# The mask's identity product of a fused attention and mixture-of-experts kernel, in four tiles of 32 rows

## Chip, cores and metric

The kernel runs on one core of a Trainium2 chip. The metric is the time of one execution on the device in microseconds (us). TensorE is called PE below, its weight loads PEld; VectorE is DVE, ScalarE ACT, GpSimd POOL, and SyncE, which issues most DMAs, SP.

## What is computed

Attention over 8 batches with 8 heads of 576 tokens and 64 dimensions, masked to a window, then a mixture of 8 experts with a capacity of 80 tokens each:

```python
scores = scale * np.matmul(q, k.transpose(0, 1, 3, 2))
mask_plain = (rel >= 0) & (rel < window)                                  # window 32, heads 0 to 3
mask_dil = (rel >= 0) & (rel < window * dilation) & (rel % dilation == 0) # dilation 4, heads 4 to 7
scores = np.where(masks[None, :, :, :], scores, -1000000000.0)
attn = softmax(scores)
x = np.matmul(attn, v)            # 4608 tokens of 512
...
logits = x @ w_gate               # one expert per token, the 80 best tokens of each
h = np.maximum(x[tok_idx] @ w1[e], 0.0)
out[tok_idx] = gate_w[tok_idx, None] * (h @ w2[e])
```

(`attn = softmax(scores)` stands for the four lines of the maximum, exponential, sum and division.)

## The kernel before

The attention is cut into 36 tiles. One tile holds four blocks of 32 queries for each of the two kinds of heads; the 128 partitions are four groups g of 32, and on the free axis lie 4 blocks j x 2 heads x 64 keys, 512 columns of f32, one bank of PSUM (tag `sc`, three of them). Since a query sees only 32 keys back (for dilated heads in reordered positions), 64 keys suffice.

For each tile t, `scores(t)` issues two things on PE. First the mask: `identb`, a 128x128 identity in bf16, times `mask`, a bf16 tile of 0 and -8e9 with 4 x 64 columns that is read twice by a broadcast over the two heads. This product (line 350) starts the accumulation and so writes the mask into the bank. Then 16 products of queries and keys (line 354), each 32 rows of the output by 128 columns, add the scores: for each block j the four groups g. In f32 each of them is two records of PE and two of PEld in the profile.

After it come `smax` (DVE, maximum per row, line 360), `sneg` (POOL), `sexp` (ACT, eight exponentials, line 368), `ptrans` (DVE, transposes in 32x32, line 373), `pv` (PE, weights times values; line 405 for the regular tiles, 416 for the last ones), `raw` (ACT copies out of PSUM, line 425), `norm_r` and `norm` (DVE and POOL, lines 429 to 436), `xtrans` (PE transposes with the f32 identity, line 442), and copies on ACT. x goes to DRAM by a DMA on SP.

Between the tiles PE also does the routing of batches that are complete: `gate` (lines 521 to 542), `counts` (comparing keys: `KLp`, line 638, and `csp`, line 690) and `merge` (lines 754 to 801). After the last tile the routing of the last batch runs alone, with `warm` products (line 289) in between, and thirteen `fill` products of 512 columns. Then come the experts (line 1089), with their weights loaded ahead.

The order on every engine is fixed in the program: a planner (`drive`) takes from the chains of tiles and batches whichever step has the lowest cost by a table of estimated durations. In it `scores` is one step of PE. Queries, keys, values, masks and weights are loaded by SP at fixed places of that order (`before_scores`, `after_scores`).

Of the kernel before, what the change touches and what calls it, by code (L numbers as in the profile page):

```python
# [27 lines left out]
P = 128  # L28
# [91 lines left out]
def moe_attn_kernel(ctx: ExitStack, tc: tile.TileContext, io, dims, sig):  # L120
    nc = tc.nc
# [3 lines left out]
    NG = H // 2  # L125
    NT = N // P
    TPP = 2 * S // P
# [12 lines left out]
    out = io["out"]  # L140
# [8 lines left out]
    def const(name, dt=F32, pool=None):  # L149
        a = io[name]  # L150
        return (pool or cp).tile(list(a.shape), dt, name=f"c_{name}")
# [100 lines left out]
    with ExitStack() as c2:  # L252
# [13 lines left out]
        mask = kp.tile([P, TPP, 4, 64], BF16, name="mask")  # L266
        identb = const("identb", BF16, kp)
# [54 lines left out]
        t = 0  # L322
        while t < NT:
# [5 lines left out]
            t = e  # L329
# [16 lines left out]
        def scores(t):  # L346

            q = q2[t // 2 % NQ][:, t % 2]
            ps = ps2.tile([P, 4, 2, 64], F32, tag="sc", name=f"sc_{t}", bufs=3)
            nc.tensor.matmul(out=ps, lhsT=identb, rhs=mask[:, t % TPP].unsqueeze(2).broadcast_to([P, 4, 2, 64]), start=True, stop=False, skip_group_check=True)  # L350
            for j in range(4):
                for g in range(NG):
                    b, k = qplan[t][g // 2][j]
                    nc.tensor.matmul(out=ps[32 * g:32 * g + 32, j], lhsT=q[:, g, 32 * j:32 * j + 32], rhs=k2[b % 2][:, :, g, 32 * k:32 * k + 64],  # L354
                                     start=False, stop=True, skip_group_check=True)
            st[t] = {"sc": ps.rearrange("p j h c -> p (j h) c")}
# [547 lines left out]
        def tile_chain(t):  # L904
# [5 lines left out]
            e = yield "PE.sc", d_sc, max(qstart.get(t, 0.0), E_(("ex", t - 3)) + lat)  # L910
            before_scores(t)
            scores(t)
            after_scores(t)
            ev["sc", t] = e
# [126 lines left out]
        t = ps1.tile([P, 512], F32, tag="lt", name="fill")  # L1041
# [252 lines left out]
```

## Time and profile before

| | |
|---|---|
| median of three runs | 313.79 us (312.93 to 313.81) |
| the profiled execution | 311.25 us |
| its span | 309.5 us |
| mean granted clock of PE | 0.987 |

The profile is of one execution. It lists what each engine did when, in us from the start of the span, and names for an idle time what ended it. In names of tiles buffer numbers are left out. A form such as 128*32 behind a PE record is the part of the array that it uses, 128 rows by 32 columns; 128x512 behind it is what is streamed through. Ends of matmuls are modelled, starts are not, so intervals between starts say more than busy time.

### The profile page before, as it was taken

What the parts mean: (1) busy time and instruction counts of PE and PEld (TensorE: products, weight loads), DVE (VectorE), ACT (ScalarE), POOL (GpSimd) and SP (SyncE); (2) the same over time, 40 slices, a digit from 0 to 9 for tenths busy, and PEclk for the clock granted to TensorE, in tenths of its full rate; (3) what the DMA queues carried; (4) which work ended last, traced back from release to release, by engine and by line L of the source; (5) the groups of instructions that cost most, each with busy time, mean ns of one, the idle gap of its engine ahead of it and who ended that gap; (6) DMA issues with size and microseconds to landing.
All of it is one profiled execution on the core that took longest, in us unless ns stands there. A gap on an engine that the chain in (4) does not pass through costs nothing. (4 is left out here: it accounts for less than half of the span.)

```text
span 309.5 us, 12133 instructions
## 1 busy us (share of the span) xinstructions
PE 285.7 (92%) x4976; PEld 201.2 (65%) x4976; DVE 133.4 (43%) x532; ACT 162.3 (52%) x602; POOL 128.5 (42%) x273
## 2 busy tenths in 40 slices
PE   7659999999999999999899888889999999999991
PEld 6435566565575656665566666654788788788791
DVE  6424444768656857567587559840000000000000
ACT  3939777767757678678556754202232332332322
POOL 9503332646376484754286662446203321110111
PEclk9779999999999999999999999999999999999999
DMA  7999989979799998999985947957999999990000
GB/s 214 272 318 300 301 312 301 359 236 317 242 309 327 294 334 257 304 360 322 321 302 158 399 145 251 344 213 208 391 400 414 389 385 391 409 384 21 23 19 26
DMA packets 30727, 87.21 MB, mean 282 GB/s; under 512 B 4304, under 2 KB 6608, under 8 KB 29776
## 3 DMA queue, kind: packets, MB, share of 16 engines
q1 hardware_dynamic: 28832, 83.55, 78.5%
q0 software_dynamic: 1280, 2.62, 2.7%
q8 instruction: 39, 0.64, 0.9%
q10 hardware_dynamic: 560, 0.26, 0.4%
q14 instruction: 16, 0.13, 0.1%
HBM read 66.23 MB, written 20.19 MB: 279 GB/s over the span
## 5 line engine op out<-in xcount | busy, mean ns | idle before, releaser
L436 POOL TENSOR_TENSOR x<-r,rc 128x256 f32<-128x256 f32 x71 | 43.5, 634 | 59.4 <-DVE rc L430 17.5
L405 PE MATMUL pv<-v,pts 128*32 128x260 f32 x992 | 65.3, 387 | 0.1
L368 ACT ACTIVATE ex<-sc,mx 128x64 f32<-128x64 f32 x288 | 62.8, 344 | 3.4 <-POOL mx L363 3.4
L1089 PE MATMUL h<-wr,xe 128*32 128x256 f32 (+1 forms) x576 | 45.4, 452 | 0.7 <-ACT xe L1086 0.4
L467 ACT COPY xT<-xt 128x256 f32<-128x256 f32 (+5 forms) x114 | 33.5, 409 | 20.3 <-PE xt L442 20.3
L354 PE MATMUL sc<-k,q 128*32 128x128 f32 x1152 | 40.3, 282 | 3.8 <-issue 2.2
L1089 PE MATMUL y<-wr,hT 128*32 128x384 f32 (+1 forms) x768 | 43.5, 379 | 0.0
L1089 PEld LDWEIGHTS y<-wr,hT 128*32 128x32 f32 x768 | 42.3, 110 | 1.2 <-issue 0.2
L373 DVE STREAM_TRANSPOSE pts<-ex 128x512 f32<-128x512 f32 x36 | 25.4, 706 | 36.7 <-PE pv L405 26.7
L1119 DVE COPY hT<-th 128x192 f32<-128x192 f32 x8 | 2.9, 357 | 86.8 <-ACT hT L1122 86.8
L405 PEld LDWEIGHTS pv<-v,pts 128*32 128x32 f32 x992 | 27.9, 109 | 17.6 <-issue 3.5
L354 PEld LDWEIGHTS sc<-k,q 128*32 128x32 f32 x1152 | 30.4, 112 | 12.8 <-issue 8.3
L1144 POOL DMA_INDIRECT out<-yo,itok x8 | 7.4, 928 | 68.3 <-ACT yo L1141 51.7
L1089 PEld LDWEIGHTS h<-wr,xe 128*32 128x32 f32 x576 | 26.5, 110 | 13.7 <-ACT h L1107 0.8
L425 ACT COPY r<-pv 128x260 f32<-128x260 f32 x72 | 27.4, 425 | 14.3 <-PE pv L405 12.7
L360 DVE TENSOR_REDUCE mx<-sc 128x8 f32<-128x512 f32 x36 | 24.4, 679 | 13.1 <-PE sc L354 12.9
L442 PE MATMUL xt<-c_ident,x 128*128 128x128 f32 x144 | 23.6, 285 | 0.7 <-POOL x L436 0.4
L1138 ACT ACTIVATE yo<-y,gsel 80x384 f32<-80x384 f32 x8 | 4.6, 577 | 33.9 <-PE y L1089 33.9
L245 POOL DMA_INDIRECT xg<-xs,irow x16 | 15.6, 974 | 15.1 <-PE tx L1083 6.1
L442 PEld LDWEIGHTS xt<-c_ident,x 128*128 128x128 f32 x144 | 15.2, 141 | 8.2 <-issue 3.7
L717 POOL TENSOR_SCALAR or<-c_pack,rr 80x80 bf16<-80x80 f32 x40 | 18.8, 485 | 3.9 <-DVE rr L735 3.9
L289 PE MATMUL warm<-ones 128*128 128x128 bf16 x181 | 16.1, 241 | 2.9 <-DVE zero L837 1.1
(132 smaller groups left out, 349.8 us busy)
## 6 DMA issues: line engine op xcount, KB each, us to landing
wr<-in_w SPq DMA_DIRECT2D x64, 512.0 KB, 10.4
v<-in_v SPq DMA_DIRECT2D x72, 144.0 KB, 5.3
out<-zero SPq DMA_DIRECT2D x18, 512.0 KB, 7.7
xs<-x SPq DMA_DIRECT2D x36, 256.0 KB, 5.7
q<-in_q SPq DMA_DIRECT2D x17, 512.0 KB, 5.7
k<-in_k SPq DMA_DIRECT2D x14, 608.0 KB, 6.9
q<-in_q SPq DMA_DIRECT2D x2, 256.0 KB, 3.7
k<-in_k SPq DMA_DIRECT2D x2, 256.0 KB, 5.2
```

Source lines behind the costliest of these rows:

```text
L289: nc.tensor.matmul(out=t[:, 0:P], lhsT=ones, rhs=ones, start=True, stop=True, skip_group_check=True)
L354: nc.tensor.matmul(out=ps[32 * g:32 * g + 32, j], lhsT=q[:, g, 32 * j:32 * j + 32], rhs=k2[b % 2][:, :, g, 32 * k:32 * k + 64], start=Fals ...
L360: nc.vector.tensor_reduce(out=st[t]["mx"], in_=st[t]["sc"], axis=AX.X, op=ALU.max)
L368: nc.scalar.activation(ex[:, n], st[t]["sc"][:, n], AF.Exp, bias=st[t]["mx"][:, n:n + 1], scale=1.0 / float(D) ** 0.5)
L373: nc.vector.transpose(out=pt.rearrange("p a b c d -> p (a b c d)"), in_=st[t].pop("ex").rearrange("p a c -> p (a c)"))
L405: nc.tensor.matmul(out=ps[32 * j:32 * j + 32], lhsT=pt[:, j, hh, half, :], rhs=vb[vt // 2 % NV][:, :, 8 * (vt % 2) + 2 * vi + hh], start=( ...
L425: nc.scalar.copy(r.rearrange("p (g h) d -> p h g d", h=2)[:, hh] if whole[t] else r[:, 4 * hh:4 * hh + 4], st[t].pop(("pv", hh)))
L436: eng.tensor_tensor(out=x[:, s_], in0=o[:, s_, 0:D], in1=rc[:, s_].unsqueeze(2).broadcast_to([P, 4, D]), op=ALU.mult)
L442: nc.tensor.transpose(out=st[t]["xt"][:, c, :], in_=x[:, c * P:(c + 1) * P], identity=ident)
L467: copy(out=dst, in_=ps[:, HC * hh:HC * hh + HC, col:col + n])
L717: nc.gpsimd.tensor_scalar(out=out[:, a], in0=iota[0:k], scalar1=r1[:, a:a + 1], scalar2=None, op0=ALU.is_equal)
L1089: nc.tensor.matmul(out=out, lhsT=x, rhs=w, start=start, stop=stop, skip_group_check=True)
```

## The change

The mask's product is issued as four, one for each group g of 32 partitions of the output. Each takes 32 columns of the identity as weights and streams the same mask, and each starts the accumulation of its own part of the bank:

```diff
             ps = ps2.tile([P, 4, 2, 64], F32, tag="sc", name=f"sc_{t}", bufs=3)
-            nc.tensor.matmul(out=ps, lhsT=identb, rhs=mask[:, t % TPP].unsqueeze(2).broadcast_to([P, 4, 2, 64]), start=True, stop=False, skip_group_check=True)
+            for g in range(NG):
+                nc.tensor.matmul(out=ps[32 * g:32 * g + 32], lhsT=identb[:, 32 * g:32 * g + 32], rhs=mask[:, t % TPP].unsqueeze(2).broadcast_to([P, 4, 2, 64]),
+                                 start=True, stop=False, skip_group_check=True)
             for j in range(4):
                 for g in range(NG):
```

The planner's table is the same, so is the order of everything else on PE and on the other four queues; lines below move by two. On PE it looks like this before, around the scores of the tile whose bank is `sc_1925` (pv are PV products, msb one of the routing; the numbers in names are the program's own):

```order
L405 MATMUL pv_1_1910<-v_2_149,pts_1712 32x260 x8
L350 LDWEIGHTS c_identb
L350 MATMUL sc_1925<-mask,c_identb 128x512
L354 MATMUL sc_1925<-k_0_143,q_0_145 32x128 x16
L769 LDWEIGHTS ohT_0_1875
```

The same place with the change, where that bank is called `sc_1988`:

```order
L407 MATMUL pv_1_1973<-v_2_149,pts_1769 32x260 x8
L351 LDWEIGHTS c_identb
L351 MATMUL sc_1988<-mask,c_identb 32x512
L351 LDWEIGHTS c_identb
L351 MATMUL sc_1988<-mask,c_identb 32x512
L351 LDWEIGHTS c_identb
L351 MATMUL sc_1988<-mask,c_identb 32x512
L351 LDWEIGHTS c_identb
L351 MATMUL sc_1988<-mask,c_identb 32x512
L356 MATMUL sc_1988<-k_0_143,q_0_145 32x128 x16
L771 LDWEIGHTS ohT_0_1938
```

One load and one product of 128 output rows have become four of each with 32; PV stands ahead of them and the scores behind, as before. Over 36 tiles these are 108 loads and 108 products more.

On PE around the `KLp` products of the first batch, before, with the mask of `sc_929` between two halves of PV:

```order
L405 MATMUL pv_1_912<-v_0_147,pts_733 32x260 x8
L350 LDWEIGHTS c_identb
L350 MATMUL sc_929<-mask,c_identb 128x512
L354 MATMUL sc_929<-k_0_143,q_1_146 32x128 x16
L405 MATMUL pv_0_960<-v_0_147,pts_807 32x260
L405 MATMUL pv_0_960<-v_1_148,pts_807 32x260 x7
L638 MATMUL KLp_0_976<-c_ident,key 128x128 x4
```

And with the change:

```order
L407 MATMUL pv_1_945<-v_0_147,pts_760 32x260 x8
L351 LDWEIGHTS c_identb
L351 MATMUL sc_962<-mask,c_identb 32x512
L351 LDWEIGHTS c_identb
L351 MATMUL sc_962<-mask,c_identb 32x512
L351 LDWEIGHTS c_identb
L351 MATMUL sc_962<-mask,c_identb 32x512
L351 LDWEIGHTS c_identb
L351 MATMUL sc_962<-mask,c_identb 32x512
L356 MATMUL sc_962<-k_0_143,q_1_146 32x128 x16
L407 MATMUL pv_0_996<-v_0_147,pts_837 32x260
L407 MATMUL pv_0_996<-v_1_148,pts_837 32x260 x7
```

`KLp` follows these rows here too: the mask, the scores and a half of PV stay between the first half of the earlier PV and it.

## Rows read from the trace of the kernel before

**Rows 1.** The page: PE's busy time and share; its granted clock in 40 slices.
```profile
PE 285.7 (92%) x4976; PEld 201.2 (65%) x4976; DVE 133.4 (43%) x532; ACT 162.3 (52%) x602; POOL 128.5 (42%) x273
...
PEclk9779999999999999999999999999999999999999
```

**Rows 2.** Table by stretches: from:to, length, busy us (records) per engine, clock, DMA.
```profile
23.00:172.00 149.00, 145.40 (x2747) 91.25 (x2750) 94.44 (x367) 106.63 (x440) 78.59 (x186) 1.00 0.91 299
172.00:208.00 36.00, 31.38 (x605) 22.87 (x592) 25.96 (x137) 14.27 (x68) 17.14 (x44) 1.00 0.76 270
208.00:309.50 101.50, 94.28 (x1424) 75.94 (x1424) 2.86 (x8) 28.36 (x65) 20.80 (x22) 0.99 0.71 265
```

**Rows 3.** PE's waits, 23 to 172 us: releaser, total us, times, longest; six rows.
```profile
PE KLp L638 <- DVE ohc L583: 1.4, 2, 0.9
...
PE lt L540 <- ACT gsb L532: 0.2, 1, 0.2
```

**Rows 4.** PE in order of time: start, length, line, operation, names, form, records.
```profile
153.90 1.97 PE L405 MATMUL pv<-v,pts 128*32 128x260 f32 x32
155.79 0.39 PE L350 MATMUL sc<-mask,c_identb 128*128 128x512 bf16 x1
156.12 1.08 PE L354 MATMUL sc<-k,q 128*32 128x128 f32 x32
157.13 0.65 PE L638 MATMUL KLp<-c_ident,key 128*128 128x128 f32 x4
157.61 0.32 PE L782 MATMUL msc<-oh,th 128*80 128x8 bf16 x5
...
159.83 1.08 PE L405 MATMUL pv<-v,pts 128*32 128x260 f32 x16
160.85 0.39 PE L350 MATMUL sc<-mask,c_identb 128*128 128x512 bf16 x1
161.17 1.08 PE L354 MATMUL sc<-k,q 128*32 128x128 f32 x32
162.07 1.06 PE L405 MATMUL pv<-v,pts 128*32 128x260 f32 x16
163.06 0.65 PE L690 MATMUL csp<-ones,gtl 128*128 128x1 bf16 x14
```

**Rows 5.** Weight loads in order of time, the same place; in brackets, idle before.
```profile
160.85 0.10 PEld L350 LDWEIGHTS <-c_identb 128*128 128x128 bf16 x1 [0.42 <-issue]
161.17 0.81 PEld L354 LDWEIGHTS sc<-k,q 128*32 128x32 f32 x32 [0.23 <-issue]
161.96 0.68 PEld L405 LDWEIGHTS pv<-v,pts 128*32 128x32 f32 x16
```

**Rows 6.** Groups by line: records, busy us, mean ns of one, idle before.
```profile
L1043 PE MATMUL fill<-gtl,ones 128*128 128x512 bf16 x13 | 3.0, 379 | 0.0
```

**Rows 7.** Mask products in order of time: the fourth, the fifth, the last but one.
```profile
18.70 0.58 PE L350 MATMUL sc<-mask,c_identb 128*128 128x512 bf16 x1 [3.48 <-DMA mask<-in_mask]
...
23.14 0.39 PE L350 MATMUL sc<-mask,c_identb 128*128 128x512 bf16 x1
...
165.65 0.39 PE L350 MATMUL sc<-mask,c_identb 128*128 128x512 bf16 x1
```

**Rows 8.** PE and DVE in order of time around one wait of PE.
```profile
50.61 1.09 PE L405 MATMUL pv<-v,pts 128*32 128x260 f32 x16
...
51.77 0.71 DVE L373 STREAM_TRANSPOSE pts<-ex 128x512 f32<-128x512 f32 x1 [3.01 <-PE pv L405]
...
54.63 0.19 DVE L583 TENSOR_TENSOR ohc<-c_pack,m 128x40 bf16<-128x40 f32 x1
...
54.86 0.40 PE L638 MATMUL KLp<-c_ident,key 128*128 128x128 f32 x2 [0.95 <-DVE ohc L583]
```

**Rows 9.** Waits of weight loads, 23 to 172 us; first and last of those counted.
```profile
PEld xt L442 <- POOL mx L363: 1.5, 3, 0.5
...
PEld L797 <- DVE rc L429: 0.2, 1, 0.2
```

## Prediction

> **What bounds the kernel now.** I read the share of each engine first, then the table by stretches, then who waited for whom, then the order of time on TensorE. TensorE (PE) is busy 92% of the span, at the full clock of 2.4 GHz in every slice after the third [rows 1]. In the stretch from 23 to 172 us, which holds 32 of the 36 tiles of attention, PE is busy 145.40 of 149 us, VectorE 94, ScalarE 107 and GpSimd 79 [rows 2]. A busy PE is no proof, since ends of matmuls are modelled; the waits are. Only 149.00 - 145.40 = 3.6 us are idle there, and the table of waits names seven of them, the longest 0.9 us, none on a DMA [rows 2, 3]. So in this stretch PE's own instruction stream sets the pace, and time taken out of it moves all that follows. After 172 us no mask product runs; that part hangs on the last tile and should only start earlier.
>
> **What a mask product costs now.** All the score, PV and gate products of this kernel use the array 32 columns wide (128*32 in the rows); the mask's product uses it whole (128*128). The order of time shows what a change of width costs [rows 4]. A PV block of 16 records that is entered and left with a change takes 159.83 to 160.85, 1.02 us. Two such blocks in a row, again entered and left with one, take 153.90 to 155.79, 1.89 us; so a block inside its own width takes 1.89 - 1.02 = 0.87. A block entered from the scores (same width) and left with a change takes 162.07 to 163.06, 0.99. Leaving therefore costs 0.99 - 0.87 = 0.12 and entering 1.02 - 0.99 = 0.03. The scores say the same: 1.01 us from 156.12 when a 128-wide product follows, 0.90 from 161.17 when PV follows, a difference of 0.11, and there both neighbours are f32, so it isn't the type of the data. The weight loads show why: those of PV begin at 161.96, 0.11 before its first matmul, under the scores, while the mask's begins at 160.85 with its own matmul, after 0.42 us in which no load ran [rows 5].
>
> From the mask's start to the first score is 0.32 us (160.85 to 161.17). Thirteen whole-width bf16 products of the same 512 columns in a row are busy 3.0 us, and one alone 0.379: (3.0 - 0.38)/12 = 0.22 us each [rows 6]. So 0.10 of the 0.32 is again the end of a width.
>
> **The change part by part.** It removes one load and one product per tile and adds four of each, 32 columns wide, each over all 512 columns. Nothing else moves: the order on all five queues stays, so no DMA passes another and no wait is added.
>
> *The product itself.* Four pieces side by side cost one piece, or four. The nearest row is the scores: 32 records of 128 columns in 0.90 us are 0.113 for each four, while four whole-width products of 128 f32 columns take 157.13 to 157.61, 0.12 each [rows 4]. Four side by side cost no more than one, so I take 0.22 us for the four pieces. They are bf16 where those rows are f32, and no row shows bf16 four wide; the bounds are 0.22 and 4 x 0.22 = 0.88.
>
> A page weighs against that. In the Trainium skill ("TensorE: Matmul & The Clock Gate", Part 3, the measured speedups) four packed pieces of 512 columns gave 3.07 and not 4 times the speed. By that, an estimate, the four would cost 0.22 x 4/3.07 = 0.29, 0.07 more per tile and 2.2 us in all; the score rows show no such loss, so my sum leaves it out.
>
> *The four weight loads.* Three more of 0.1 us per tile. I cost them at nothing, because the 128*32 loads before PV ran under the scores [rows 5]. Without that cover it is about 0.11 (four started together, by the lead of those loads) to 4 x 0.10 = 0.40 us (one after another) [rows 5].
>
> *The widths.* PV to mask no longer changes (0.12), mask to scores no longer does (0.10), the scores are entered in their own width (0.03): 0.25 us per tile; with rows rounded to 0.01 I carry 0.245. This needs a PV before the mask in the same width. That holds for the 31 masks from 23.14 to 165.65 us [rows 7]. The last one follows products in yet another form, and the four before 23 us lie in the start-up, where PE waits for loads, such as 3.48 us for the mask itself [rows 7]; these five I value at nothing, at most 0.13 each (mask to scores, and their entry) for two of them. Sum on PE: 31 x 0.245 = **7.6 us**.
>
> *What takes it back.* Where PE waits for a chain that began at an earlier PE event, a mask product between the two saves nothing; the wait grows. An example: a PV block from 50.61 releases VectorE at 51.77; a chain of 12 instructions there ends at 54.82, and PE, which has done mask, scores and another PV meanwhile, waits 0.95 us for it [rows 8]. Of the seven waits two hold no mask: 540's stands right behind 442's, and 769's chain begins after the last mask. To the five I add one that the modelled ends may hide: 6 x 0.245 = 1.5 us. Behind these stand waits that now end just before the array would feel them. The table of weight loads has 25 waits with a named producer besides DMA, from three on GpSimd's mx to one on VectorE's rc [rows 9]; six are those above, 19 are left. Each gives back between 0 and 0.245, so 0 to 4.7 us. I take five of them in full, 1.2 us, because most PE blocks between producer and use hold no mask. Net: 7.6 - 1.5 - 1.2 = **4.9 us**.
>
> The loads don't take it back by themselves: no PE wait from 23 to 172 us is on a DMA [rows 3], though the engines are 91% busy [rows 2], so loads will land with less to spare. After 208 us weights stream at 71% DMA share [rows 2]; the 36 us before run at 76%, so the buffers that are filled ahead have room to be full 5 us earlier.
>
> The profiled execution took 311.25 us with a span of 309.5; the median of the runs shown is 313.79, 0.8% above it. Taking 4.9 off gives 306.35 for a profile like this one and **308.9 us** for the median.
>
> **The rivals.**
>
> *The others become the bound.* If most of the 19 near waits, or the loads at 91%, turn into real waits, 4.7 instead of 1.2 us is given back: 7.6 - 1.5 - 4.7 = 1.4 us gained, 312.4 at the bound. For it: the DMA share, and chains on VectorE as long as that of rows 8. Against: ScalarE and VectorE have some 42 and 55 us of idle in those 149. Midway between 4.9 and 1.4 gained it gives 310.6.
>
> *The loads aren't hidden.* If the four loads must wait for the products before them, the gain per tile falls from 0.245 to 0.135 (0.11 paid): 31 x 0.135 = 4.2, less 1.5 given back in the same share as above, so 2.7 us, 311.1. One after another, 0.40, it turns: 0.155 lost on 31 tiles, 4.8 us, 318.6. The score rows speak against both, with 32 loads in 0.81 us under their own products [rows 5]. The Trainium skill (same page, Part 3, the mechanism) says that a load runs under matmuls in flight only where their row groups differ; all tiles here use all 128 rows, so by that rule this rival would win. The trace disagrees: loads of the same rows overlap.
>
> *The pieces run one after another (slower).* If bf16 pieces over one shared right-hand side don't run side by side, each tile pays 3 x 0.22 = 0.66 and saves 0.245: 0.415 x 31 = 12.9 us, 326.7. It decides as soon as pieces start more than 0.245/3 = 0.08 us apart. Against it: f32 pieces start together. For it: no bf16 row.
>
> *Nothing comes of it.* If what holds the first score is not the width but that it adds to what the mask has just written, and what holds the mask is its wait for the score buffer, the gaps stay: 313.8. Against: PV's second half adds to what its first half wrote, and its block still runs at 0.87; and the scores show the same 0.11 with another product behind.
>
> **How the numbers follow.** Forecast 308.9: 0.69. Others bind: 0.14. Loads not hidden but still a gain: 0.04; with a loss: 0.02. Pieces in a row: 0.04. Nothing: 0.07. The forecast's own range is all of its given-back term: 7.6 - 1.5 = 6.1 us gained, plus 0.26 from the two odd tiles and up to 1.5 if the six waits don't absorb: 306.0 at the low end. At the high end the range takes in the second case to its bound, 312.4. Some 0.15 lies outside. About 0.3% (0.9 us) is what a measurement of this kernel can tell from no change. Faster by more: 0.69 + 0.14 + 0.04 = 0.87. Within: 0.07. Slower: 0.06.
>
> **What would show it.** Right: from mask to first score about 0.22 instead of 0.32 us; from PV's start to the mask 0.99 or less instead of 1.02, 0.90 where the scores precede; the mask's loads beginning before its matmuls, without the 0.42 us; pieces starting within some 0.02 us; the 149 us stretch about 5 us shorter, the stretches after it as long as before; idle time in front of KLp larger. Wrong: pieces 0.1 us or more apart, loads that begin with the matmul, or a stretch that stays at 149 with new waits on VectorE, GpSimd or a load.

## The result, and the profile after

The changed kernel takes **310.81 us** in the median (309.14 to 311.52, four runs); the kernel before takes 313.80 beside it. The ratio is 0.9884, with a 95% interval of 0.9839 to 0.9929. The interval lies below 1, so it is faster, by 3.0 us where 4.9 were forecast. (A ratio compares undisturbed executions alone, a median counts all; the two can differ by some tenths of a per cent. Sessions differ too: the kernel before came to 313.8, 316.3, 316.4, 314.2 and 313.8 us in the five of this study, so times and ratios are compared only within a session. The profiles show where the sessions differ: the experts take 101.5 to 101.9 us in the profiles of three of them, 103.3 to 103.6 in those of the two with 316 us.)

PE in order of time, changed kernel, at the place of [rows 4] (start, length, line, operation, names, form, records; line 407 is PV, 351 the mask, 356 the scores):

```profile
157.32 1.08 PE L407 MATMUL pv<-v,pts 128*32 128x260 f32 x16
158.23 0.40 PE L351 MATMUL sc<-mask,c_identb 128*32 128x512 bf16 x4
158.44 1.05 PE L356 MATMUL sc<-k,q 128*32 128x128 f32 x32
159.32 1.06 PE L407 MATMUL pv<-v,pts 128*32 128x260 f32 x16
160.31 0.43 PE L692 MATMUL csp<-ones,gtl 128*128 128x1 bf16 x11
```

PV to mask is 0.91 us (1.02 in rows 4), mask to first score 0.21 (0.32), scores to PV 0.88 (0.90). Over all tiles of the steady part the median from mask to first score is 0.215 us, 0.320 before. The four pieces together are busy 0.40 us, as long as the one product was; in the first tiles of the steady part they start 0.001 to 0.024 us apart. The weight loads in order of time, some eleven microseconds earlier in the same kernel, against [rows 5]:

```profile
146.61 0.12 PEld L351 LDWEIGHTS <-c_identb 128*32 128x32 bf16 x4
146.83 0.45 PEld L356 LDWEIGHTS sc<-k,q 128*32 128x32 f32 x12
```

The four loads of the mask start at 146.61, before the first piece at 146.83, and the bracket with 0.42 us of idle time is gone. Over the 31 tiles of the steady part the loads start 0.217 us ahead of the mask's first piece in the median; before it was 0.004.

The table by stretches, as in [rows 2] (from:to, length, busy us and records of PE, PEld, DVE, ACT, POOL, then clock, DMA share, GB/s):

```profile
23.00:172.00 149.00, 141.14 (x2907) 96.26 (x2900) 96.08 (x378) 107.98 (x448) 78.88 (x187) 1.00 0.93 307
172.00:208.00 36.00, 31.30 (x545) 23.14 (x548) 24.09 (x125) 12.88 (x60) 17.39 (x42) 0.95 0.66 239
```

PE is busy 4.3 us less in the first stretch, and its clock in the second is 0.95 where it was 1.00. Since the work shifts against fixed times, I measure from mask to mask: from the fifth (23.14 us in [rows 7]) to the last of the 36, from there to the first product of the experts, and from that to the end.

| profiled run | start of 5th mask | 5th to last mask | last mask to experts | experts | span |
|---|---|---|---|---|---|
| before | 23.14 | 145.53 | 39.26 | 101.53 | 309.47 |
| changed | 24.13 | 141.35 | 41.64 | 101.51 | 308.64 |

The attention gained 4.2 us. The start lost 1.0 and the stretch between attention and experts 2.4, so that this one execution gained 0.8.

Where the 2.4 went, in order of time of PE in the changed kernel (line 418 is PV of the last tiles, 444 the transposes of x, 289 the warming products, 523 the gate):

```profile
168.51 1.17 PE L418 MATMUL pv<-v,pts 64*32 64x130 f32 x64
171.81 0.60 PE L444 MATMUL xt<-c_ident,x 128*128 128x128 f32 x4 [2.13 <-issue]
172.24 0.32 PE L784 MATMUL msc<-oh,th 128*80 128x8 bf16 x5
173.45 2.14 PE L289 MATMUL warm<-ones 128*128 128x128 bf16 x18 [0.88 <-ACT xT L469]
175.51 1.94 PE L523 MATMUL lt<-xT,wg 128*32 128x128 f32 x32
```

and in the kernel before:

```profile
171.83 1.59 PE L416 MATMUL pv<-v,pts 64*32 64x130 f32 x64
173.35 0.65 PE L442 MATMUL xt<-c_ident,x 128*128 128x128 f32 x4
...
175.04 1.60 PE L289 MATMUL warm<-ones 128*128 128x128 bf16 x18 [0.88 <-ACT xT L467]
176.57 1.08 PE L521 MATMUL lt<-xT,wg 128*32 128x128 f32 x32
```

PE stands 2.13 us ahead of xt with no producer named ("issue"), where before the PV ahead of it is 0.42 us longer than its 1.17 and nothing else is lost: 1.7 us. Then the granted clock falls to 1.2 GHz for a while and the 32 gate products take 1.94 us instead of 1.08, 0.9 us; the 18 warming products ahead of them lose another 0.5 (2.06 to the next row, 1.53 before). Together this is more than the 2.4, so some 0.7 of it doesn't reach the experts. The prediction had none of it.

The longest waits of PE from 23 to 172 us in the changed kernel, against [rows 3]:

```profile
PE xt L444 <- issue: 2.1, 1, 2.1
PE KLp L640 <- DVE ohc L585: 1.6, 2, 1.1
PE KLp L640 <- DVE key L579: 0.8, 1, 0.8
PE xt L444 <- POOL x L438: 0.7, 1, 0.7
...
```

KLp on ohc went from 1.4 to 1.6 us. Ahead of KLp's first transposes PE lost in all 2.4 us before and 3.2 after, by the intervals between starts.

### The profile page after: what moved, and what is told of

It reads as the page before. It is cut to its first block, busy times and chain, and to the rows that moved or that the text cites. A ratio compares the mean times of both kernels' runs of the same rounds, so it can differ in the third digit from the quotient of the medians.

```text
span 308.6 us, 12348 instructions
## 1 busy us (share of the span) xinstructions
PE 280.4 (91%) x5083; PEld 206.1 (67%) x5084; DVE 133.1 (43%) x532; ACT 161.7 (52%) x602; POOL 128.2 (42%) x273
## 5 line engine op out<-in xcount | busy, mean ns | idle before, releaser
L407 PE MATMUL pv<-v,pts 128*32 128x260 f32 x992 | 67.0, 393 | 0.5 <-issue 0.4
L356 PE MATMUL sc<-k,q 128*32 128x128 f32 x1152 | 39.1, 277 | 2.8 <-POOL mx L365 1.7
L356 PEld LDWEIGHTS sc<-k,q 128*32 128x32 f32 x1152 | 33.5, 112 | 10.1 <-POOL mx L365 2.1
L351 PE MATMUL sc<-mask,c_identb 128*32 128x512 bf16 x144 | 14.8, 391 | 5.0 <-DMA mask<-in_mask 5.0
```

The lines of the kernel that those rows point to most:

```text
L407: nc.tensor.matmul(out=ps[32 * j:32 * j + 32], lhsT=pt[:, j, hh, half, :], rhs=vb[vt // 2 % NV][:, :, 8 * (vt % 2) + 2 * vi + hh], start=( ...
```

## Experiments

### The changed kernel twice more, and the theory

My theory after the result: (1) the saving per tile is as predicted; (2) waits for chains of other engines take part of it back, as predicted; (3) what is missing comes from how the program is fetched. The profile's table of queues has one that carries instructions. Changed kernel:

```profile
q8 instruction: 40, 0.66, 0.9%
```

That is 40 packets of 0.0165 MB, 16 KB; there were 39 before. TensorE's stream, matmuls and weight loads together, had 2 x 4976 = 9952 instructions [rows 1], 39 packets of 256; the change adds 36 x 6 = 216, which makes 40. So, by this count, a packet holds 256 instructions, 128 products with their loads, and after the masks every border between two packets lies at another product than before. In the trace the long PE waits without a producer have such a packet beside them: PE goes on 2.2 to 2.5 us after the packet's start (169.39 to 171.81 here, 137.77 to 140.31 earlier in this run). Over all fourteen profiles this holds for each of the 32 waits of more than 0.25 us between 23 us and the last tile's PV; the few in the experts, of 0.30 to 0.44 us, have no such packet beside them. The Trainium skill ("Runtime: NRT & Kernel Launch", Instruction fetch mechanics) says that instructions arrive in blocks of 16 KiB, 256 at a time, and that crossing a border is mostly hidden. The block size agrees with the packets. Mostly hidden agrees too: of the 38 packets that start after 23 us in this run, two leave a wait of more than 0.25 us. But one of the two is 2.13 us long.

The rival: the missing gain is chance, or the DMA and the clock.

> The changed kernel once more, unaltered. Theory A (PE saved some 0.22 us per tile from 23 us on, 4.2 us in all, and lost 2.1 us again in one wait near 171.8 us, in front of the transposes, for its own instructions, which come in blocks of 256 whose borders 216 more instructions have moved): the wait of about 2 us stands at the same transposes again, and the ratio is 0.987 to 0.992. Rival B (that wait, and the half-clock stretch behind it, were chance in one execution): no such wait, and the median is nearer 309.

Measured: 313.94 us against 316.27, ratio 0.9928 (0.9897 to 0.9960). Its profile has the same wait at the same xt, but 0.36 us long, and another of 0.60 further on, and no half clock there:

```profile
170.22 0.60 PE L444 MATMUL xt<-c_ident,x 128*128 128x128 f32 x4 [0.36 <-issue]
...
176.24 0.41 PE L418 MATMUL pv<-v,pts 64*32 64x130 f32 x3 [0.60 <-issue]
```

> The changed kernel, once more and unchanged, in the same session as the version with both steps. If the filling and the swap are real gains, it comes out as in the two sessions before, 0.988 to 0.994 of the kernel before, and above the version with both steps by 2.5 us or more; if their better ratios belonged to the sessions, it comes within 1 us of it.

Measured: 311.74 against 314.24, ratio 0.9935 (0.9901 to 0.9970). The same two places again, now 1.02 and 1.15 us:

```profile
169.27 0.60 PE L444 MATMUL xt<-c_ident,x 128*128 128x128 f32 x4 [1.02 <-issue]
...
175.84 0.41 PE L418 MATMUL pv<-v,pts 64*32 64x130 f32 x3 [1.15 <-issue]
```

The two waits of this run are 128 products apart in the trace, one block. The place is a property of the program, the length one of the execution. In this third profile no such wait falls between the fifth and the last mask, and that stretch is 140.73 us, 4.80 less than before. In the first two it is 141.35 and 142.06, 4.2 and 3.5 less; tile by tile, what they have more than the third lies around such waits (at 140.3 us in the first; at 35.6 and 43.0 in the second). So the third is the cleanest picture of the change, but the best of three too, and its spacing from mask to mask can be set beside the kernel before tile by tile:

| difference, changed less before | tiles (5th mask on) | sum, us |
|---|---|---|
| -0.24 or -0.25 us | 16 of 31 | -3.9 |
| -0.04 to +0.06 (all given back) | 8 | 0.0 |
| longer, +0.39 and +0.21 (a wait grew by more) | 2 | +0.6 |
| -0.13 to -0.17, next to start or end | 3 | -0.5 |
| -0.43 and -0.62 | 2 | -1.05 |

(In the tile of -0.62 the kernel before lost some 0.36 us of its own at 43.8 us, which the run keys_later_before below lacks; without it the stretch is 4.4 us shorter and not 4.8.) A tile that saves all and one that saves nothing, kernel before:

```profile
115.85 0.39 PE L350 MATMUL sc<-mask,c_identb 128*128 128x512 bf16 x1
...
120.48 0.39 PE L350 MATMUL sc<-mask,c_identb 128*128 128x512 bf16 x1
...
129.35 0.39 PE L350 MATMUL sc<-mask,c_identb 128*128 128x512 bf16 x1
...
132.18 0.77 PE L442 MATMUL xt<-c_ident,x 128*128 128x128 f32 x4
...
135.02 0.39 PE L350 MATMUL sc<-mask,c_identb 128*128 128x512 bf16 x1
```

and the third run of the changed kernel:

```profile
112.99 0.40 PE L351 MATMUL sc<-mask,c_identb 128*32 128x512 bf16 x4
...
117.39 0.40 PE L351 MATMUL sc<-mask,c_identb 128*32 128x512 bf16 x4
...
125.76 0.40 PE L351 MATMUL sc<-mask,c_identb 128*32 128x512 bf16 x4
...
128.53 0.96 PE L444 MATMUL xt<-c_ident,x 128*128 128x128 f32 x4
...
131.44 0.39 PE L351 MATMUL sc<-mask,c_identb 128*32 128x512 bf16 x4
```

The first interval is 4.63 and then 4.40 us. The second is 5.67 and 5.68: there xt, whose x comes from POOL, takes 0.96 instead of 0.77 us, and the rest goes in gaps of some hundredths beside it. No row of waits names these. That they are the near waits of the prediction, become real, fits these rows, but no run isolates it.

### Is it the width, or the splitting?

```diff
-            for g in range(NG):
-                nc.tensor.matmul(out=ps[32 * g:32 * g + 32], lhsT=identb[:, 32 * g:32 * g + 32], ...
+            for g in range(2):
+                nc.tensor.matmul(out=ps[64 * g:64 * g + 64], lhsT=identb[:, 64 * g:64 * g + 64], ...
```

> The mask's product in two tiles of 64 rows instead of four of 32. If what is saved is the change of width between the mask and its neighbours (theory A), nothing is saved: 0.31 to 0.32 us from mask to first score, and a time within 2 us of before. If splitting into pieces as such saved it (pieces that start while others end), the mask to first score falls to about 0.22 and the steady stretch is 4 us shorter as with four.

Measured: 318.02 against 316.27, ratio 1.0061 (1.0030 to 1.0093). Order of time on PE:

```profile
157.05 0.41 PE L351 MATMUL sc<-mask,c_identb 128*64 128x512 bf16 x2
157.39 1.08 PE L356 MATMUL sc<-k,q 128*32 128x128 f32 x32
```

From mask to score it is 0.34 us again, and the loads of the two pieces start with the first piece (0.002 us ahead in the median), as those of the whole product did. Pieces of 64 rows cost what the whole product cost and a little more. So splitting alone brings nothing; having the scores' own width does.

### How much of a TensorE time per tile reaches the end?

```diff
             for g in range(NG):
                 nc.tensor.matmul(out=ps[32 * g:32 * g + 32], ..., start=True, stop=False, skip_group_check=True)
+            for g in range(NG):
+                nc.tensor.matmul(out=ps[32 * g:32 * g + 32], ..., start=False, stop=False, skip_group_check=True)
```

> The changed kernel with its four mask products of a tile issued a second time, added on top (the mask enters the scores twice; since it is 0 or a very negative number the probabilities stay as they are). It adds one width-matched set of four products per tile, 0.215 us by the changed kernel's own step from mask to first score (158.23 to 158.44), so 31 x 0.215 = 6.7 us of TensorE time between the fifth mask and the last, and asks how much of a TensorE time per tile reaches the end. Theory (TensorE's order sets the pace of this stretch, but its waits for other engines take part of any change back): the waits, about 7.1 us of the changed kernel against 4.2 of the one before, shrink again by 2 to 3 us, so the stretch from the fifth mask to the last mask grows from about 142 to 145.5 to 146.5, and the median comes to 0.998 to 1.006 of the kernel before. Rival 1 (all of it lies on the path): 148.5 or more, ratio 1.010 to 1.015. Rival 2 (another engine sets the pace): the stretch stays at 142 to 143, ratio as for the changed kernel alone (0.988 to 0.993).

Measured: 315.22 against 316.36, ratio 1.0007 (0.9964 to 1.0050); fifth to last mask 144.89 us. Order of time:

```profile
150.24 0.40 PE L351 MATMUL sc<-mask,c_identb 128*32 128x512 bf16 x4
150.45 0.40 PE L354 MATMUL sc<-mask,c_identb 128*32 128x512 bf16 x4
150.66 1.06 PE L359 MATMUL sc<-k,q 128*32 128x128 f32 x32
```

A second set costs its 0.21 us, 6.7 on 31 tiles, and 144.89 - 140.73 = 4.2 us of that arrive, against the third profile of the changed kernel (neither of the two has a long border wait in this stretch). All 16 tiles that were shorter by 0.24 or 0.25 us there are longer by 0.21 or 0.22 here, and the two that had grown by 0.39 and 0.21 shrink by 0.31 and 0.17. The waits at KLp shrink from 3.2 to some 2.3. This is a little under the 145.5 that I expected, and neither rival. So some 60% of a time that is spread over the tiles reaches the end of this stretch; 4.8 of the 7.6 us saved are 63%, or 58% without the 0.36 that the kernel before lost by itself. The two agree, from either side.

### Are KLp's waits what can be had back?

```diff
-                for a in range(-(-hd // P)):
-                    spread(c0 + a, a * P)
+                def heads():
+                    for a in range(-(-hd // P)):
+                        spread(c0 + a, a * P)
+                if last:
+                    heads()
+                else:
+                    held.append(heads)      # issued after pv(t, 1), or just ahead of the copy of KL
...
```

> The changed kernel with the four key transposes (KLp) of batches 0 to 4 held back on TensorE until behind the next group of products (xt, or PV's second half); no work is added or left out, and the order of all other groups stays. In the changed kernel TensorE stands 3.2 us at these five places (1.28, 0.25, 0.67 and 1.00 us at the four largest), against 2.4 in the kernel before. Theory (what the change gives back is lost at such waits): they fall to under 1.2 us, and the stretch from the fifth mask to the last falls from about 142 us by 1.5 to 2.5 us; ratio to the kernel before 0.980 to 0.987. Rival (the waits are only where the chains of other engines show; freed of one, TensorE stands at the next, or VectorE, whose count work now comes later in its fixed order, delays the softmax): the stretch stays within 0.7 us of 142, ratio 0.988 to 0.994.

Measured: 313.40 against 316.36, ratio 0.9862 (0.9806 to 0.9917); fifth to last mask 142.68. The ratio falls in the theory's range and the stretch in the rival's. The profile tells why. Around the largest wait, third run of the changed kernel:

```profile
54.04 0.62 PE L640 MATMUL KLp<-c_ident,key 128*128 128x128 f32 x4 [1.11 <-DVE ohc L585]
54.50 0.60 PE L444 MATMUL xt<-c_ident,x 128*128 128x128 f32 x4
```

and with the keys later:

```profile
36.22 0.42 PE L356 MATMUL sc<-k,q 128*32 128x128 f32 x7 [1.02 <-issue]
...
56.16 0.44 PE L444 MATMUL xt<-c_ident,x 128*128 128x128 f32 x2 [0.35 <-POOL x L438]
56.81 0.44 PE L444 MATMUL xt<-c_ident,x 128*128 128x128 f32 x2 [0.21 <-POOL x L438]
57.09 0.60 PE L640 MATMUL KLp<-c_ident,key 128*128 128x128 f32 x4
```

KLp waits no more, but xt in its place waits for x. Tile by tile, the swap takes 0.39, 0.42, 0.24 and 0.04 us out of four tiles and adds 0.32 to a fifth: 0.8 us of the 3.2. The rest of the difference in the stretch is two waits without a producer (the 1.02 us above and one of 1.22 at 44.4 us); the run again has shorter ones at the same two places (0.47 and 0.40 us), without the step. So the rival holds for most of it: PE freed of one wait stands at the next.

> The kernel before with the same step alone: its four key transposes of a batch held back behind the next group of products. Its waits there were 2.4 us. Theory that these waits are what lies on the path: the stretch from the fifth mask to the last falls from 145.5 us by 1.0 to 2.0 us, and the ratio is 0.993 to 0.997; the changed kernel with this step then stands below this one by more than the 3.4 to 4.2 us that the change brings without it, by some 4.5 us, because less of it is given back. Rival that the waits only move: within 0.5 us of 145.5, ratio 0.998 to 1.002.

Measured: 314.32 against 316.36, ratio 0.9978 (0.9938 to 1.0018); fifth to last mask 143.88, 1.65 us less than before. The stretch is in the theory's range and the ratio in the rival's. Some 0.36 of the 1.65 are that loss at 43.8 us that this run lacks, so the step is worth 1.3 us here against 0.8 in the changed kernel. The part of my theory that said the change would gain more with the swap (4.5 us) is not borne out.

### Where the blocks of instructions end

One step of 20 products (40 instructions) moves every later border by 20 products. The kernel before and the changed one differ by 108 products ahead of the last tiles, so 20 more in the changed kernel make a whole block of 128 products and bring the borders back to where they were; 20 fewer in the kernel before put them where the changed one has them. Warming products at the start were cut in half or joined, or small ones were added:

```diff
-            for _ in range(n):
+            for i in range(n + (20 if n == W0 else 0)):     # aligned: 20 of 128 columns, 40 of 64
...
+            for i in range(n - (20 if n == W0 else 0)):     # shifted_before: 20 of 256 columns
...
+            for i in range(n + (20 if n == W1 else 0)):     # pad_at_warm: 20 of 16 columns added
...
+            m, c = (n + 128, 32) if n == W0 else (n, P)     # whole_block: 168 of 32 x 32
```

> The change with 40 PE instructions more at the start: 40 of the 128-column warming products become 20 of 128 and 40 of 64 columns, the same columns in all. 216 + 40 = 256, so that in the last tiles the borders of instruction blocks lie at the same instructions as before the change. A: the wait near 171.8 us and the half-clock stretch behind it are gone, some 2 to 3 us less than the changed kernel, about 308, ratio 0.980. B or any cause in the data: the same as the changed kernel, 310.8.

> The kernel before with 40 PE instructions fewer at the start: the 40 warming products of 128 columns become 20 of 256, the same columns. -40 and +216 differ by 256, so the borders of instruction blocks in the last tiles lie where the change puts them. A: a wait of about 2 us with no releaser appears in front of the transposes of the same tile (near 173 us, after the PV of line 416), and the time is 1.5 to 3 us longer than before. B: as before, within 0.5 us.

> The changed kernel with 20 more warming products of 16 columns (40 TensorE instructions) in the second warming call, ahead of the third tile's scores, where TensorE waits for q anyway. From there on every 16 KB block of instructions starts at the same instruction as in the kernel before, as it did in the run aligned, but the filling stands in another place and the start is as in the changed kernel. Theory (where the block borders fall decides part of the time; the changed kernel loses by the move of 216 instructions): ratio to the kernel before 0.976 to 0.985, as in aligned, and below the repeat of the changed kernel in the same session. Rival (the better ratio of aligned came from its start or from the spread of the runs): ratio 0.988 to 0.996, as for the changed kernel repeated.

> The changed kernel with 128 more warming products in its first warming call (168 products of 32 x 32 in place of 40 of 128 x 128): 256 more TensorE instructions, one whole 16 KB block, so that every later instruction lies at the same place in its block as in the changed kernel itself, not as in the kernel before. Theory (the place of the borders is what the filled versions gained by): no gain, ratio to the kernel before 0.988 to 0.996 when the start costs what it did, and above the version with 20 filling products of the same session by 2 us or so. Rival (any added warming products help): 0.980 to 0.987. If the 168 products take longer than the 4.45 us of the 40, the fifth mask starts later by that much, and it is taken off.

> The changed kernel with the 20 filling products of 16 columns in the second warming call, unchanged from the run pad_at_warm, in the same session as the whole block. Theory: 0.980 to 0.988 again. Rival (its first ratio was luck): 0.989 to 0.995.

| run | borders as in | ratio to the kernel before (95%) | executions in the ratio | median less before's, us |
|---|---|---|---|---|
| changed, again, changed_third | changed | 0.9884, 0.9928, 0.9935 (each within 0.984 to 0.997) | 4, 10, 10 | -3.0, -2.3, -2.5 |
| whole_block | changed | 0.9925 (0.9880 to 0.9970) | 8 | -1.5 |
| aligned | before | 0.9804 (0.9752 to 0.9856) | 3 | -4.7 |
| pad_at_warm | before | 0.9842 (0.9794 to 0.9889) | 6 | -4.5 |
| pad_again | before | 0.9898 (0.9817 to 0.9979) | 3 | -2.9 |
| shifted_before | changed | 1.0104 (1.0061 to 1.0148) | 9 | +1.9 |

The rows show the border itself. It is the first wait without a producer after 168 us. In the run shifted_before it stands ahead of xt, where the kernel before has none:

```profile
172.66 1.17 PE L417 MATMUL pv<-v,pts 64*32 64x130 f32 x64
175.07 0.60 PE L443 MATMUL xt<-c_ident,x 128*128 128x128 f32 x4 [1.24 <-issue]
```

In aligned it stands 20 products earlier, inside the PV of 64 records, 45 + 19:

```profile
170.57 0.91 PE L419 MATMUL pv<-v,pts 64*32 64x130 f32 x45
172.86 0.63 PE L419 MATMUL pv<-v,pts 64*32 64x130 f32 x19 [1.37 <-issue]
```

and in whole_block, 128 products further on, it is back ahead of xt:

```profile
170.91 1.17 PE L419 MATMUL pv<-v,pts 64*32 64x130 f32 x64
173.89 0.60 PE L445 MATMUL xt<-c_ident,x 128*128 128x128 f32 x4 [1.81 <-issue]
```

pad_at_warm and pad_again split the same PV at the same record (1.10 and 0.71 us). That a border of 128 products stands there, and that it moves with the count, is shown. What it does to the time is less firm. Beside each other in one session, the changed kernel came out 2.3 us better with the old borders (aligned) than with its own (again), and the kernel before lost 1.9 us with the borders of the changed one. But aligned's six executions, 307.8 to 315.4 us, overlap the twelve of again, 310.4 to 318.1, and its profile has the wait (the 1.37 us above) and the half clock behind it all the same, where A expected both gone. pad_at_warm ran in a session without the changed kernel, so its ratio is set beside those of other sessions only. pad_again falls in its rival's range and can't be told from the changed kernel; beside it whole_block is 1.4 us longer in the median, with intervals that overlap. And pad_at_warm's own profile has two more such waits inside the attention, as

```profile
56.46 0.60 PE L408 MATMUL pv<-v,pts 128*32 128x260 f32 x2 [1.68 <-issue]
```

Which borders cost, and why the same one costs 0.36 us in one execution and 2.13 in another, stays open. The warming products change the start as well: the fifth mask starts at 23.8 to 25.6 us in the profiles of these five runs, at 23.3 to 24.1 in the three of the changed kernel. For whole_block that is 1.5 to 2.3 us, so its -1.5 says little by itself.

### Both steps

> The changed kernel with both steps of the runs before: the key transposes held back behind the next group, and the 20 filling products in the second warming call. Theory (waits at the key transposes and the place of the instruction blocks' borders are two separate losses): the two gains add, some 2 us each against the changed kernel alone, so 0.976 to 0.982 of the kernel before, with no wait of TensorE for the key transposes over 0.3 us and a stretch from the fifth mask to the last of 140 to 141.5 us. Rival (they are one loss, or the filling only moves a border from one place to another and the swap uses the same slack): 0.983 to 0.988, as with either step alone.

Measured: 308.95 us against 314.24, ratio 0.9831 (0.9777 to 0.9885), and 2.8 us below the changed kernel of the same session (changed_third, 0.9935). It beats both kernels. The two gains don't add to the 0.976 to 0.982 of the theory; 0.9831 is in the rival's range, at its edge. No wait at KLp is left in the attention, and the stretch is 141.14 us with one border wait in it.

## Why the prediction was right, and where it wasn't

The median of 310.81 us is faster, as forecast, and inside the range of 306.0 to 312.4; it lies 1.9 us above the 308.9.

- **PE's stream sets the pace of the attention.** Right, with a limit: some 60% of a time per tile reaches the end, from both sides (4.8 of 7.6 us saved in the third profile, 4.2 of 6.7 added).
- **0.245 us per tile.** Right: 16 of 31 tiles are shorter by 0.24 or 0.25. It lies where it was put: 0.11 at the end of PV, 0.105 between mask and score, 0.02 at the end of the scores. Pieces of 64 rows save nothing.
- **Four bf16 pieces cost one, and the loads nothing.** Right; 0.21 us for the four, as much again for a second set, and loads that begin 0.2 us ahead. So the rivals of loads in the open and of pieces in a row fall. The two rules of the Trainium skill that the prediction weighed ("TensorE: Matmul & The Clock Gate", Part 3) don't show here. The four pieces take 0.215 us and not the estimate of 0.29; the 3.07 behind it is the page's figure for pieces packed by rows, while these lie side by side in columns. And loads of the same rows do overlap, by 0.217 us.
- **Given back 2.7 us.** Right in size. Ten tiles of 31 gave all of it back (eleven were taken), two of them more; the sum is 7.6 - 4.8 = 2.8 us in the third profile, 3.4 and 4.1 in the first two with their border waits. Its cause is bounded, not isolated: with KLp's waits moved away only 0.8 us came back.
- **The rival that others become the bound.** It did not happen: at 93% DMA share no PE wait of the attention is on a load, and 3.5 to 4.8 us of the stretch were gained where it allowed 1.4. The median of 310.81 lies next to this rival's 310.6 and not to the 308.9, but the profiles don't show its mechanism: no wait there is on a load, and in the first profile 3.4 of the 4.2 us gained in this stretch were lost again outside it.
- **"The stretches after it as long as before", and no price for 108 more products in the stream.** This is the step that failed, as far as the profiles show. The stretch to the experts was 2.4, 0.0 and 1.2 us longer (41.64, 39.27 and 40.49) in the three profiles of the changed kernel than in the one of the kernel before. The prediction counted the added instructions as time on the array and in the loads; that they move the borders of the 16 KB blocks was not in the sum. The waits at borders of 0.4 to 2.1 us each and the half clock behind the longest are of the size of what is missing between 4.9 and the 2.3 to 3.0 us measured, but that they are its cause is argued, not shown. The granted clock is the other candidate. Over the fourteen profiles this stretch took 39.3 to 40.5 us in the four in which the clock stayed at 2.4 GHz through it (before, again, changed_third, pad_at_warm), 40.4 to 42.5 in the seven with some 3 to 7 us at 1.2 GHz, and 44.1 to 45.0 in the three with more than 10; one of these three, keys_later_before, has the mask as before. The start differed by 0.2 to 1.0 us as well; in the profile with 1.0 the mask came later and a longer spell at 1.2 GHz lay over the first PV. No experiment took these apart.

## What to carry to other kernels

When products of one width of the array stand among those of another, price both changes of width from the rows (here 0.11 and 0.10 us) and ask whether the odd one can be cut to its neighbours' width: here the pieces ran side by side at the price of one (0.215 us against 0.22). Expect about what the waits of the stretch allow, not the whole: a second set of the same products tells the share that reaches the end. And when an edit changes the number of instructions of a long unrolled stream, compare it with a version in which filling brings later code back to its old place in the 16 KB blocks; moving the borders of the kernel before went with a ratio of 1.0104, so a difference of 0.5% may belong to that and not to the edit.

## What the runs showed of the hardware that I had not expected

- TensorE sometimes stands at a border of instruction blocks (two of 38 in the first profile of the changed kernel). The places lie 128 products, so 256 instructions, apart and are fixed in a program: the wait at one and the same product was 0.36, 1.02 and 2.13 us in three executions. TensorE went on 2.2 to 2.5 us after the block's packet had started.
- After the 2.13 us wait the granted clock fell from 2.4 to 1.2 GHz (1.94 us for 32 gate products that took 1.08); after those of 0.36 and 1.02 us at the same place it stayed. It is no simple rule: it also fell in mask_twice after a wait of 0.49 and in pad_again after one of 0.71, and not in pad_at_warm after one of 1.10.
- A mask product over 128 rows and 64 columns of the array, next to products of 32 columns, loses as much as one over the whole array (0.34 against 0.32 us from mask to score).
